# First loads on a second queue, the correction column inside the warm-up, bias rows mirrored at once, and VectorE's half evictions put behind the next minima

## The chip, the cores and the metric

The kernel runs on one core of a Trainium2 chip. The metric is the device time of one execution in microseconds, median of the runs shown. The engines are TensorE (PE in the profile, its weight loads PEld), VectorE (DVE), ScalarE (ACT), GpSimd (POOL) and SyncE (SP), which here only issues transfers. TensorE's clock has two levels in the records, 1.2 and 2.4 GHz; the profile gives it as a share of full, 0.50 or 1.00.

## What is computed

An attention layer with a learned bias over relative positions, followed by two gated feed-forward layers. Batch 2, 8 heads, 576 positions, head size 64; the layers have 1152 tokens, width 512, inner width 1536. Cut to what matters:

```
psi_rel = log1p(|i - j|);  psi_i = log1p(max(i, 1))
x       = psi_rel / psi_i                         # 576 x 576
h       = max(x * w1 + b1, 0)                     # 32 hidden values for each i, j
bias    = h @ w2                                  # one value for each head, i, j
scores  = q @ k.T / 8 + bias
p       = exp(scores - rowmax);  p = p / (rowsum + 1e-9)
y       = p @ v
y       = (sigmoid(y @ w_gate) * (y @ w_val)) @ w_out             # first layer
y       = rmsnorm(y) ... (silu(y @ w_gate) * (y @ w_val)) @ w_out  # second layer
```

## The kernel before

Every engine's instructions are in the order in which the program writes them; nothing is reordered. The work comes in four stages: a warm-up with the first loads, a prelude that makes bias rows, the attention loop, and the two feed-forward layers.

**Loads.** At the start SP issues, in this order: the first part of the table of log distances (`w1l`, four parts), the parameters `prms`, the per-position column `bpr`, the factors `nip`, the table's second part, then the q and k tiles `raw` of four (batch, head pair) combinations, each as two transfers of 64 partitions (one half holds one head; which half comes first alternates with the batch, `half`), and the table's last two parts. VectorE multiplies the table by `w1` (`table`), and `bpr` by `b1` into `bpc`; GpSimd does the same for its own use into `nbpc`.

**Warm-up.** TensorE runs 11 products of a tile of ones (line 133). After them come two tiny products (line 694) of the weights with the column b1, the *correction column*: rows whose hidden values GpSimd made are short of a constant, which VectorE copies into `corr` (lines 695 and 696) and which is added when a bias row is evicted.

**Bias rows.** The 576 positions i are cut into 36 groups T of 16. For a group, four tiles of hidden values `ht` are made (`bias_h`, lines 212, 214 and 216, split over ScalarE, GpSimd and VectorE), then TensorE multiplies them by w2 (`bias_mm`, line 234), and the PSUM result is scaled and shifted into a tile `be`. Because the bias depends on |i - j|, only the wider side of a row is computed; the other side is its mirror image (`bias_end`, lines 258 and 260, on ScalarE for the first 16 groups and on GpSimd for the rest), after which SP stores the tile in DRAM (`bias_d`, line 264). Groups wider than 512 columns are computed in two halves; ScalarE evicts both (line 239), except in groups 0 to 3, where VectorE evicts the second half (line 243). `bias_step` does one step of this pipeline: hidden values of one group, products of the group before, mirror and store of the group before that. So a group is mirrored one step after its eviction. 16 groups are made in the prelude (18 steps), with `qk_mm(0)` and the first bias load after step 9; the other 20 inside the loop. Groups are taken in the order 18 to 23, 16, 17, 8 to 15, 0 to 7, 24 to 35. The pools hold 12 tiles of hidden values, 8 of `be` and 4 PSUM banks for single products.

**Attention loop.** A unit n is one batch, two heads and a block of 128 rows i. For each unit and head, TensorE makes scores (`qk_mm`, line 334, issued one unit ahead), VectorE adds the bias tile `bt` and takes the row minimum of the negated sum (`reduce_min`, line 344, "the minima"), ScalarE takes exponentials (`expo`, line 363), VectorE or GpSimd normalizes (`normal`), TensorE transposes (`transp`, line 390) three units later and multiplies by v (`pv`, line 425). There are two double banks for scores, so the scores of unit n+1 wait for the minima of unit n. The bias tile comes back from DRAM (`load_bias`, line 305) on SP's queue and waits for the stores of its block's eight groups. The order within a unit is a string of letters: M0 and M1 are the minima, X0 and X1 the exponentials, N the normalization of the unit before, Q the next scores, T, E0 to E2 the transposes and their evictions, A, b and c a `bias_step` (two of them in units 0 to 4), B the feeding of bias tiles, L loads, P0, P1 and V the products with v. For units below 20 it is

```
"M0 M1 T X0 N Q E0 E2 E1 A L X1 P0 P1 b c B V"
```

Groups 0 to 3, those with VectorE's half evictions, have their products in units 0 (one), 1 (two) and 2 (one). A half eviction stands in VectorE's queue right behind the hidden values of the next group, and ahead of the next unit's minima or of one more group's hidden values.

Of the kernel before, what the change touches and what calls it, by code (L numbers as in the profile page):

```python
# [13 lines left out]
ALU = mybir.AluOpType  # L14
# [3 lines left out]
B, H, S, D = 2, 8, 576, 64  # L18
# [11 lines left out]
WARM = 11  # L30
SCALE = 1.0 / 8.0
# [8 lines left out]
NORM_DVE = range(6)  # L40

BIAS_HALF_DVE = (0, 1, 2, 3)
PRE = 16

MIRROR_ACT = 16
# [10 lines left out]
LASTV = {22 + i: (i % 2, i // 2) for i in range(8)}  # L56

ORDERS = [
# [3 lines left out]
]  # L62
# [11 lines left out]
def groups_of(it):  # L74
    a, r = BLK[it]
    return range(a // 16, (a + r) // 16)
# [11 lines left out]
def fused_kernel(ctx: ExitStack, tc: tile.TileContext, qk, vp, tab, pcol, invp, prm, wts, rg, out):  # L88
    nc = tc.nc
# [8 lines left out]
    def bank(nm):  # L98
        return ps1.tile([128, 512], F32, tag="one", name=nm)
# [10 lines left out]
    w1l = bp.tile([128, TABW], F32, name="w1l")  # L110
# [3 lines left out]
    corr = bp.tile([128, 3], F32, name="corr")  # L114
    nip = bp.tile([128, 36], F32, name="nip")
    prms = bp.tile([128, 34], F32, name="prms")
    ones = const.tile([128, 128], F32, name="ones")
# [1 line left out]
    nc.vector.memset(corr, 0.0)  # L119

    PARTS = [slice(192, S), slice(S, 1024), slice(0, 192), slice(1024, TABW)]
    nc.sync.dma_start(w1l[:, PARTS[0]], tab[:, PARTS[0]])
    nc.sync.dma_start(prms, prm)
    nc.sync.dma_start(bpr, pcol)
    nc.sync.dma_start(nip, invp)
    ident = const.tile([128, 128], F32, name="ident")
    make_identity(nc, ident)
    rgs = const.tile([128, NCC], F32, name="rgs")


    warm = bank("warm")
    for _ in range(WARM):
        nc.tensor.matmul(warm[:, :128], ones, ones, start=True, stop=True)

    bias_d = [dram.tile([rows_of(i) * H + H, bias_width(i)], F32, name=f"bias_d{i}") for i in range(5)]
# [7 lines left out]
    def half(b, h):  # L143
        x = (h + b) % 2 * 64
        return slice(x, x + 64)

    def load_raw(b, hp):
        t = wk.tile([128, 2, S], F32, tag=f"raw{hp // 2}", name=f"raw{b}{hp}", bufs=4)
        raws[b, hp] = t
        for h in range(2):  # L150
            r = half(b, h)
            nc.sync.dma_start(t[r], qk[b, hp][:, r, h].rearrange("w p s -> p w s"))

    vs = {}

# [24 lines left out]
    nc.sync.dma_start(w1l[:, PARTS[3]], tab[:, PARTS[3]])  # L180
    nc.gpsimd.tensor_scalar(nbpc, bpr, prms[:, 1:2], -1.0, op0=ALU.mult, op1=ALU.mult)
    nc.vector.tensor_scalar(bpc, bpr, prms[:, 1:2], None, op0=ALU.mult)

    def table(i):
        x = w1l[:, PARTS[i]]
        nc.vector.tensor_scalar(x, x, prms[:, 0:1], None, op0=ALU.mult)
# [34 lines left out]
    def bias_mm(T):  # L221
        hs = hts.pop(T)
        c0, w = span(T)
        right = T * 16 + 15
        if GORDER.index(T) in SPARE:
            be = wk.tile([128, 2 * S], F32, tag="raw1", name=f"be{T}", bufs=4)[:, : S + 15]
        else:
            be = bp.tile([128, S + 15], F32, tag="be", name=f"be{T}", bufs=8)
        o = right + c0
        cut = w if w <= 512 else w // 2  # L230
        for a in range(0, w, cut):
            ps = bank(f"bps{T}_{a}")
            for cg in range(4):
                nc.tensor.matmul(  # L234
                    ps[cg * 32 : cg * 32 + 32, :cut], prms[:, 2:34], hs[cg][:, a : a + cut], start=True, stop=True
                )
            off = corr[:, pooled[T] : pooled[T] + 1]
            if not (a and T in BIAS_HALF_DVE):
                nc.scalar.activation(
                    be[:, o + a : o + a + cut], ps[:, :cut], AF.Identity, bias=off, scale=nip[:, T : T + 1]  # L240
                )
            else:
                nc.vector.tensor_scalar(
                    be[:, o + a : o + a + cut], ps[:, :cut], nip[:, T : T + 1], off, op0=ALU.mult, op1=ALU.add
                )
        bes[T] = be

    def bias_end(T):
        be = bes.pop(T)
        c0, w = span(T)  # L250
        right = T * 16 + 15
        if c0 == 0:
            src, dst = be[:, right + 1 : 2 * right + 1][:, ::-1], be[:, :right]
        else:
            k = S - 1 - 16 * T
            src, dst = be[:, right - k : right][:, ::-1], be[:, right + 1 : right + 1 + k]
        if GORDER.index(T) < MIRROR_ACT:
            nc.scalar.activation(dst, src, AF.Copy)
        else:
            nc.gpsimd.tensor_scalar(dst, src, 1.0, 1.0, op0=ALU.mult, op1=ALU.mult)  # L260
        it = IT_OF[T]
        a = sum(BLK[it]) - 1 - right
        r = (T - groups_of(it)[0]) * 128
        nc.sync.dma_start(bias_d[it][r : r + 128, a : a + S + 15], be)
        stored.append(T)

    GORDER = [T for it in ITS for T in groups_of(it)]
    GORDER = GORDER[2:8] + GORDER[:2] + GORDER[8:]
    hq, mq, eq = list(GORDER), [], []


    def bias_step(more=True):
        m, e = mq[:1], eq[:1]
        if hq and more:
            T = hq.pop(0)
            bias_h(T, *BIAS_H[GORDER.index(T)])
            mq.append(T)
        for T in m:
            bias_mm(mq.pop(0))
            eq.append(T)  # L280
        for T in e:
            bias_end(eq.pop(0))


# [28 lines left out]
    def feed_bias(last, wait=0):  # L313
        while ahead and ahead[0] <= last:
            it = UNITS[ahead[0]][2]
            seen = stored[: len(stored) - wait]
            if any(T not in seen for T in groups_of(it)):
                return
            load_bias(ahead.pop(0))
# [369 lines left out]
                idle += 1  # L689


    cps = bank("cps")
    for c in (64, 96):
        nc.tensor.matmul(cps[c : c + 32, :1], prms[:, 2:34], prms[:, 1:2], start=True, stop=True)
    nc.vector.tensor_scalar(corr[96:, 1:2], cps[96:, :1], 1.0 / SCALE, None, op0=ALU.mult)
    nc.vector.tensor_scalar(corr[64:, 2:3], cps[64:, :1], 1.0 / SCALE, None, op0=ALU.mult)
    for i in range(PRE + 2):
        bias_step(i < PRE)
        if i == 3:
# [8 lines left out]
    for n in range(NU + TL + 1):  # L708
        if n == NU:
            attn.close()  # L710
            open_ring("me", range(EARLY, EARLY + MORE), "left")
        ev = []
        on_dve = (2,) if n < NBIAS or n >= NU else (1, 2)

        def evac(i):
            if len(ev) > i:
                if i in on_dve:
                    nc.vector.tensor_copy(*ev[i])
                else:
                    nc.scalar.activation(*ev[i], AF.Copy)  # L720

        def load_new():
            if n in LOADR:
                load_raw(*LOADR[n])
            if n in LOADV:
                load_v(*LOADV[n])
            if n in LASTV:
                load_last(*LASTV[n])

        live = n < NU  # L730
        nb = BSTEPS.get(n, 0)
        acts = {
            "M0": lambda: live and reduce_min(n, 0),
            "M1": lambda: live and reduce_min(n, 1),
            "X0": lambda: live and expo(n, 0),
            "X1": lambda: live and expo(n, 1),
            "T": lambda: 0 <= n - TL < NU and ev.extend(transp(n - TL)),
            "E0": lambda: evac(0),
            "E1": lambda: evac(1),
            "E2": lambda: evac(2),  # L740
            "N": lambda: 0 <= n - 1 < NU and normal(n - 1),
            "C": lambda: n >= NBIAS + LAG and advance(EARLY if live else EARLY + MORE, 1 if live else 2),
            "B": lambda: live and feed_bias(n + 4),
            "A": lambda: nb > 1 and bias_step(),
            "c": lambda: nb > 2 and bias_step(),
            "b": lambda: nb and bias_step(),
            "L": load_new,
            "Q": lambda: n + 1 < NU and qk_mm(n + 1),
            "P0": lambda: drain(peq, 3),
            "P1": lambda: drain(peq, 2),  # L750
            "V": lambda: 0 <= n - TL < NU and pv(UNITS[n - TL]),
        }
        for x in ORDERS[0 if n < NBIAS else 1 if live else 2].split():
            acts[x]()
        if n == NBIAS - 1:
            assert not eq
            prod.close()
            open_ring("mc", range(EARLY), "right")
            fetch()
        if n >= NU:  # L760
            advance(EARLY + MORE, 1)
        if n == NU:
            while (0, 0, 1) not in wp:
                advance(EARLY + MORE, 1)
            gate_val(0)
# [3 lines left out]
    for s in range(EARLY + MORE, RING):  # L769
        tag, size = ("pt", 9 * 128) if s < EARLY + MORE + 2 else ("v", 1024)  # L770
        t = w2.tile([128, size], F32R, tag=tag, name=f"wv{s}", bufs=2 if tag == "pt" else 8)
# [4 lines left out]
    for s in range(NS + 2):  # L776
# [9 lines left out]
        for half in range(2):  # L786
# [6 lines left out]
            if half == 0:  # L793
                if s < NS and not closing(s - 2):
                    low_part(s)
                if s > 1:
                    l, _, _, f = STEPS[s - 2]
# [5 lines left out]
                while norm_queue and norm_queue[0][0] <= s:  # L803
                    _, c, stage, box = norm_queue.pop(0)
# [71 lines left out]
```

## Time and profile before

| | us |
|---|---|
| median of 3 runs | 651.62 |
| lowest and highest | 650.72, 652.21 |
| the profiled execution | 651.69 |
| its span, first to last instruction | 649.9 |
| TensorE busy in the span | 637.6 |
| VectorE, ScalarE, GpSimd busy | 487.3, 352.6, 210.5 |

The profiled execution is within 0.1 us of the median, so its rows can be taken for the kernel's time as they are. Some 1.8 us lie around the span. The mean granted clock of TensorE is 0.989 of full. A group's idle time counts only where its engine holds up the others; the rows below say for each wait what ended it.

### The profile page before, as it was taken

What the parts mean: (1) busy time and instruction counts of PE and PEld (TensorE: products, weight loads), DVE (VectorE), ACT (ScalarE), POOL (GpSimd) and SP (SyncE); (2) the same over time, 40 slices, a digit from 0 to 9 for tenths busy, and PEclk for the clock granted to TensorE, in tenths of its full rate; (3) what the DMA queues carried; (4) which work ended last, traced back from release to release, by engine and by line L of the source; (5) the groups of instructions that cost most, each with busy time, mean ns of one, the idle gap of its engine ahead of it and who ended that gap; (6) DMA issues with size and microseconds to landing.
All of it is one profiled execution on the core that took longest, in us unless ns stands there. A gap on an engine that the chain in (4) does not pass through costs nothing.

```text
span 649.9 us, 11776 instructions
## 1 busy us (share of the span) xinstructions
PE 637.6 (98%) x4450; PEld 575.7 (89%) x4450; DVE 487.3 (75%) x972; ACT 352.6 (54%) x745; POOL 210.5 (32%) x237
## 2 busy tenths in 40 slices
PE   8889999999999999999999999999999999999997
PEld 5235766777799999999999999999999999999997
DVE  6869798688969987889887888787877878431322
ACT  4749888888885663454534545454555535111110
POOL 5401577566664332243322321010323423100000
PEclk9969999999999999999999999999999999999999
DMA  8865956683323342433333410211423322000111
GB/s 190 284 221 174 234 152 210 185 288 103 85 58 126 128 120 79 127 100 106 121 97 98 130 65 34 66 66 32 121 91 115 98 97 66 1 1 1 49 49 48
DMA packets 28472, 71.73 MB, mean 110 GB/s; under 512 B 3840, under 2 KB 6912, under 8 KB 28416
## 3 DMA queue, kind: packets, MB, share of 16 engines
q1 hardware_dynamic: 27552, 69.80, 35.5%
q10 hardware_dynamic: 864, 1.18, 0.5%
q8 instruction: 35, 0.57, 0.4%
q14 instruction: 21, 0.17, 0.1%
HBM read 57.72 MB, written 13.25 MB: 109 GB/s over the span
## 4 chain that ended last, share of the span: by engine, by line
PE 93%; DVE 1%; issue 1%; ACT 0%; DVEq 0%
PE gv L526 47%; PE s L334 7%; PE pv L425 6%; PE tp L390 6%; PE bps L234 3%; PE acc122a L556 1%; PE acc102b L556 1%; PE acc100b L556 1%; PE acc121b L556 1%; PE acc101b L556 1%; PE acc120b L556 1%; PE acc030b L556 1%; PE acc032b L556 1%; PE acc112b L556 1%; PE acc111b L556 1%; PE acc110b L556 1%
## 5 line engine op out<-in xcount | busy, mean ns | idle before, releaser
L503 POOL TENSOR_TENSOR ff<-ff,wr 128x512 int32<-128x512 int32 x72 | 114.1, 1585 | 256.9 <-DVE ff L502 132.9
L532 DVE TENSOR_TENSOR g<-gv,sg 128x384 f32<-128x384 f32 x72 | 40.1, 556 | 90.9 <-PE gv L526 76.9
L534 ACT ACTIVATE gh<-g 128x384 fp32r<-128x384 f32 x72 | 37.8, 525 | 99.2 <-DVE g L532 99.2
L526 PE MATMUL gv<-nh,wv 128*128 128x384 f32 x288 | 76.5, 337 | 0.0
L526 PE MATMUL gv<-xh,wh 128*128 128x384 f32 x216 | 73.2, 339 | 0.0
L526 PE MATMUL gv<-xl,wh 128*128 128x384 f32 x216 | 72.9, 337 | 0.0
L526 PE MATMUL gv<-xh,wl 128*128 128x384 f32 x216 | 72.8, 337 | 0.0
L493 DVE TENSOR_SCALAR ff<-wr 128x512 uint32<-128x512 uint32 x72 | 63.2, 877 | 0.0
L530 ACT ACTIVATE sg<-gv 128x384 f32<-128x384 f32 x72 | 34.5, 479 | 44.8 <-PE gv L526 44.8
L344 DVE CUSTOM_DVE_ANT_0 t<-s,bt 128x576 f32<-128x576 f32 x72 | 51.4, 751 | 9.6 <-PE s L334 7.6
L363 ACT ACTIVATE p<-t,mn 128x576 f32<-128x576 f32 x72 | 55.2, 767 | 4.1 <-DVE mn L344 4.1
L334 PE MATMUL s<-raw 64*128 64x288 f32 (+1 forms) x320 | 49.7, 439 | 5.7 <-issue 3.2
L507 ACT ACTIVATE wh<-ab 128x512 fp32r<-128x512 f32 x42 | 26.5, 631 | 52.2 <-DVE ab L506 51.8
L216 DVE TENSOR_SCALAR ht<-w1l,bpc 128x304 f32<-128x304 f32 (+17 forms) x100 | 53.0, 593 | 0.1
L526 PEld LDWEIGHTS gv<-nh,wv 128*128 128x128 f32 x288 | 52.4, 188 | 0.0
L540 DVE TENSOR_TENSOR gl<-g,gh 128x384 fp32r<-128x384 f32 x72 | 45.5, 631 | 7.0 <-ACT gh L534 7.0
L506 DVE SCALAR_TENSOR_TENSOR ab<-ab,ff 128x512 f32<-128x512 f32 x72 | 49.3, 685 | 1.2 <-POOL ff L503 1.2
L502 DVE SCALAR_TENSOR_TENSOR ff<-wr,ff 128x512 uint32<-128x512 uint32 x72 | 49.8, 692 | 0.0
L377 POOL TENSOR_SCALAR p<-p,rs 128x576 f32<-128x576 f32 x60 | 48.5, 820 | 2.2 <-DVE rs L372 2.2
L526 PE MATMUL gv<-nh,wh 128*128 128x384 f32 x144 | 48.7, 338 | 0.0
L526 PE MATMUL gv<-nl,wh 128*128 128x384 f32 x144 | 48.6, 337 | 0.0
L526 PE MATMUL gv<-nh,wl 128*128 128x384 f32 x144 | 48.6, 337 | 0.0
(363 smaller groups left out, 1569.9 us busy)
## 6 DMA issues: line engine op xcount, KB each, us to landing
wr<-wts SPq DMA_DIRECT2D x72, 512.0 KB, 3.6
bias_d<-be SPq DMA_DIRECT2D x36, 295.5 KB, 4.2
bt<-bias_d SPq DMA_DIRECT2D x16, 576.0 KB, 5.0
raw<-qk SPq DMA_DIRECT2D x16, 288.0 KB, 6.9
v<-vp SPq DMA_DIRECT2D x8, 320.0 KB, 4.0
bt<-bias_d SPq DMA_DIRECT2D x8, 144.0 KB, 2.9
out<-part SPq DMA_DIRECT2D x6, 192.0 KB, 1.8
out<-part ACTq DMA_DIRECT2D x6, 192.0 KB, 1.9
```

Source lines behind the costliest of these rows:

```text
L216: nc.vector.tensor_scalar(ht, src, bpc[:, t : t + 1], 0.0, op0=ALU.add, op1=ALU.max)
L334: nc.tensor.matmul(dst[:, hf, :288], raw[r, 0, r0 : r0 + rows], raw[r, 1, cs], start=True, stop=True)
L344: nc.vector.tensor_tensor_reduce(t, sp[:, :, :288], bt[:, 0 if UNITS[n][0] is None else j].rearrange("p (a c) -> p a c", a=2), -SCALE, 3.0e38,
L363: nc.scalar.activation(p[:, j], t.rearrange("p a c -> p (a c)"), AF.Exp, bias=mn[:, j : j + 1], scale=-1.0, accum_out=sm[:, j : j + 1],)
L377: nc.gpsimd.tensor_scalar(p[:, j], p[:, j], rs[:, j : j + 1], 1.0, op0=ALU.mult, op1=ALU.mult)
L493: nc.vector.tensor_scalar(ff, hw, 3, 0x3FFFFFFF, op0=ALU.logical_shift_left, op1=ALU.bitwise_and)
L502: nc.vector.scalar_tensor_tensor(ff, hw, 0xC0000000, ff, op0=ALU.bitwise_and, op1=ALU.bitwise_or)
L503: nc.gpsimd.tensor_tensor(ff.bitcast(I32), ff.bitcast(I32), lw.bitcast(I32), op=ALU.add)
L506: nc.vector.scalar_tensor_tensor(ab, ab, TINY_HI, ff.bitcast(F32), op0=ALU.is_ge, op1=ALU.mult)
L526: nc.tensor.matmul(ps[:, :CH], wt[:, cs], xt[:, cc, :], start=(k == 0), stop=(k == 11))
L540: nc.vector.tensor_tensor(gl, g32, gh.bitcast(F32), op=ALU.subtract)
L556: nc.tensor.matmul(dst, st_[:, m * 128 : m * 128 + 128], mv, start=(head and k == 0), stop=(last and k == 2))
```

## The change

Four edits. First, the table's first part, the factors `nip`, and the second half of each of the four early q and k loads are issued by ScalarE's queue instead of SP's. Second, the correction column's two products come after 5 of the 11 warm-up products, and VectorE's two copies of it right after the scaling of `bpr`. Third, the first 16 groups are mirrored and stored in the same step as their eviction. Fourth, VectorE's half evictions are put on a list, which is worked off at the start of the next `bias_step` or at a new letter D, behind the two minima, whichever comes first. The diff:

```
-    "M0 M1 T X0 N Q E0 E2 E1 A L X1 P0 P1 b c B V",
+    "M0 M1 D T X0 N Q E0 E2 E1 A L X1 P0 P1 b c B V",
...
-    nc.sync.dma_start(w1l[:, PARTS[0]], tab[:, PARTS[0]])
+    nc.scalar.dma_start(w1l[:, PARTS[0]], tab[:, PARTS[0]])
     nc.sync.dma_start(prms, prm)
     nc.sync.dma_start(bpr, pcol)
-    nc.sync.dma_start(nip, invp)
+    nc.scalar.dma_start(nip, invp)
...
-    for _ in range(WARM):
+    for _ in range(WARM // 2):
+        nc.tensor.matmul(warm[:, :128], ones, ones, start=True, stop=True)
+    cps = bank("cps")
+    for c in (64, 96):
+        nc.tensor.matmul(cps[c : c + 32, :1], prms[:, 2:34], prms[:, 1:2], start=True, stop=True)
+    for _ in range(WARM - WARM // 2):
         nc.tensor.matmul(warm[:, :128], ones, ones, start=True, stop=True)
...
-            nc.sync.dma_start(t[r], qk[b, hp][:, r, h].rearrange("w p s -> p w s"))
+            q = nc.scalar if h and hp < 2 else nc.sync
+            q.dma_start(t[r], qk[b, hp][:, r, h].rearrange("w p s -> p w s"))
...
     nc.vector.tensor_scalar(bpc, bpr, prms[:, 1:2], None, op0=ALU.mult)
+
+    nc.vector.tensor_scalar(corr[96:, 1:2], cps[96:, :1], 1.0 / SCALE, None, op0=ALU.mult)
+    nc.vector.tensor_scalar(corr[64:, 2:3], cps[64:, :1], 1.0 / SCALE, None, op0=ALU.mult)
...
-                nc.vector.tensor_scalar(
-                    be[:, o + a : o + a + cut], ps[:, :cut], nip[:, T : T + 1], off, op0=ALU.mult, op1=ALU.add
-                )
+                late.append((be[:, o + a : o + a + cut], ps[:, :cut], nip[:, T : T + 1], off))
...
+    late = []
+
+    def bias_rest():
+        while late:
+            nc.vector.tensor_scalar(*late.pop(0), op0=ALU.mult, op1=ALU.add)
...
     def bias_step(more=True):
+        bias_rest()
...
         for T in e:
             bias_end(eq.pop(0))
+        if eq and GORDER.index(eq[0]) < AT_ONCE:
+            bias_end(eq.pop(0))
...
-    cps = bank("cps")
-    for c in (64, 96):
-        nc.tensor.matmul(cps[c : c + 32, :1], prms[:, 2:34], prms[:, 1:2], start=True, stop=True)
-    nc.vector.tensor_scalar(corr[96:, 1:2], cps[96:, :1], 1.0 / SCALE, None, op0=ALU.mult)
-    nc.vector.tensor_scalar(corr[64:, 2:3], cps[64:, :1], 1.0 / SCALE, None, op0=ALU.mult)
...
+            "D": bias_rest,
```

`AT_ONCE` is 16.

## Rows read from the trace of the kernel before

**Rows 1.** Windows of TensorE: stretch, us, busy (instructions), clock, DMA share, GB/s.

```profile
0.00:55.00 55.00, 46.28 (x293) 0.88 0.79 233
55.00:650.00 595.00, 591.31 (x4159) 1.00 0.32 99
```

**Rows 2.** Windows of units 0, 1, 2: PE, PEld, DVE, ACT, POOL, clock, DMA.

```profile
28.77:34.63 5.86, 4.42 (x24) 1.63 (x24) 4.49 (x11) 3.94 (x9) 0.22 (x1) 0.68 1.01 369
34.63:42.69 8.06, 6.30 (x40) 3.11 (x40) 6.05 (x18) 3.99 (x8) 0.48 (x2) 0.59 0.73 235
42.69:49.74 7.05, 6.20 (x40) 3.08 (x41) 5.44 (x17) 3.99 (x8) 0.26 (x1) 0.76 0.40 132
```

**Rows 3.** Timeline of VectorE: start, us, line, operation, [idle before <- releaser].

```profile
34.14 0.58 DVE L243 TENSOR_SCALAR be<-bps,nip,corr 128x288 f32<-128x288 f32 x1 [1.37 <-ACT be L239]
...
40.51 0.57 DVE L243 TENSOR_SCALAR be<-bps,nip,corr 128x280 f32<-128x280 f32 x1 [1.94 <-PE bps L234]
...
48.11 0.55 DVE L243 TENSOR_SCALAR be<-bps,nip,corr 128x264 f32<-128x264 f32 x1 [1.54 <-PE bps L234]
```

**Rows 4.** Timeline of VectorE from the start to the first minima.

```profile
4.23 0.29 DVE L182 TENSOR_SCALAR bpc<-bpr,prms 128x144 f32<-128x144 f32 x1 [3.23 <-DMA bpr<-pcol]
4.44 0.55 DVE L186 TENSOR_SCALAR w1l<-w1l,prms 128x384 f32<-128x384 f32 x1
6.36 0.16 DVE L695 TENSOR_SCALAR corr<-cps 32x1 f32<-32x1 f32 x1 [1.37 <-PE cps L694]
...
6.75 3.56 DVE L216 TENSOR_SCALAR ht<-w1l,bpc 128x304 f32<-128x304 f32 x10
...
28.77 0.76 DVE L344 CUSTOM_DVE_ANT_0 t<-s,bt 128x576 f32<-128x576 f32 x1 [1.94 <-DMA bt<-bias_d]
```

**Rows 5.** Timeline of SP's queue: start, us until the last issue's end.

```profile
1.65 0.42 SPq L124 DMA_DIRECT2D bpr<-pcol  x1
...
11.36 9.43 SPq L264 DMA_DIRECT2D bias_d<-be  x8
```

**Rows 6.** Transfers issued at 1.65, 20.47 and 24.49: KB, us to landing.

```profile
bpr<-pcol SPq DMA_DIRECT2D x1, 72.0 KB, 2.5
...
bias_d<-be SPq DMA_DIRECT2D x1, 295.5 KB, 3.9
...
bt<-bias_d SPq DMA_DIRECT2D x1, 576.0 KB, 4.3
```

**Rows 7.** Timeline of TensorE: warm-up, scores at half and at full clock.

```profile
1.05 5.06 PE L133 MATMUL warm<-ones 128*128 128x128 f32 x22 [1.05 <-DVE corr L119]
...
35.49 2.93 PE L334 MATMUL s<-raw 64*128 64x288 f32 x8 [1.48 <-issue]
...
50.56 1.91 PE L334 MATMUL s<-raw 64*128 64x288 f32 x8 [0.48 <-DVE mn L344]
```

**Rows 8.** Timeline of ScalarE: evictions 8 and 9, and the mirror behind the ninth.

```profile
17.01 0.60 ACT L239 ACTIVATE be<-bps,corr,nip 128x304 f32<-128x304 f32 x1 [0.35 <-PE bps L234]
...
19.39 0.72 ACT L239 ACTIVATE be<-bps,corr,nip 128x448 f32<-128x448 f32 x1 [1.46 <-PE bps L234]
20.01 0.43 ACT L258 ACTIVATE be<-be 128x287 f32<-128x287 f32 x1
```

**Rows 9.** Windows: early half loads, a 128-partition load, two later half loads.

```profile
8.00:15.00 7.00, 6.84 (x54) 3.41 (x52) 7.00 (x17) 4.33 (x10) 5.09 (x8) 1.00 1.05 219
...
42.44:43.21 0.77, 0.00 (x0) 0.00 (x0) 0.77 (x2) 0.00 (x0) 0.00 (x0) 1.00 1.01 387
83.50:84.40 0.90, 0.90 (x11) 0.17 (x10) 0.90 (x4) 0.59 (x2) 0.08 (x1) 1.00 0.98 278
```

**Rows 10.** Windows of TensorE: the two spells at half clock.

```profile
30.90:41.10 10.20, 8.72 (x52) 0.50 0.79 265
...
44.60:48.00 3.40, 3.40 (x26) 0.50 0.31 97
```

More of the change, by code (lines that the diff above doesn't have):

```diff
@@ L42 @@
 BIAS_HALF_DVE = (0, 1, 2, 3)
+AT_ONCE = 16
 PRE = 16
```

## The prediction

> **What bounds the kernel now.** I read the page first, then the busy time by stretches, then the three iterations at the seam by timelines, then the loads. TensorE is what the time consists of: from 55 us on it is busy 591.31 of 595 us at the full clock, while in the first 55 us it is busy only 46.28 and its granted clock averages 0.88 [rows 1]. So whatever makes the first 55 us shorter should come off the end, and the change touches only that part. There the reader should see two things. Units 0, 1 and 2 of the attention loop take 5.86, 8.06 and 7.05 us, with VectorE idle 1.4 to 2.0 us in each [rows 2]; the idle time stands in front of the half evictions of line 243, 1.37, 1.94 and 1.54 us [rows 3]. VectorE runs into an eviction whose product TensorE has not finished, and the next minima, which TensorE's next scores wait for, stand behind it. And before unit 0, VectorE computes hidden rows without a pause from 6.75 to 26.83 and then waits 1.94 us for the first bias tile [rows 4].
>
> **Start of VectorE.** Constants and correction column. The column operand bpr is issued at 1.65 us and lands 2.5 later; the scaling that needs it starts at 4.23 [rows 4 to 6]. With the table's first part gone to ScalarE's queue, bpr moves up one issue slot, 0.47 us, so the scaling can start at 3.76. Before, VectorE scaled, prepared the table (0.55) and then stood 1.37 us until the correction product at the end of the warm-up was there, and started the first hidden row at 6.75 [rows 4]. Now that product sits behind 5 of 11 warm-up products: 1.05 + 5/11 of 5.06 = 3.35 us [rows 7], so it is there when VectorE asks. The new order is scaling 0.21, two corrections 0.20 each, table 0.55: 3.76 + 0.21 + 0.40 + 0.55 = 4.9. If the new traffic on the second queue delays bpr by the slot that it gained, 5.4. I take 5.05: 1.7 us sooner. The 20.1 us of hidden rows then end at 25.1 instead of 26.83. The other six warm-up products end about 0.3 us later than before, at 6.4, still ahead of the old start of bias products.
>
> **First bias tile.** Before, the eight stores are issued from 11.36 to 20.47 [rows 5]; the last lands 3.9 us after its issue and the bias tile 4.3 us after its own [rows 6]: 20.5 + 3.9 + 4.3 = 28.7, which is the 28.77 of the first minima. "Mirrored at once" sends each store when its own eviction is done and not one row later: the eighth eviction starts at 17.01 [rows 8], now 15.3, with its 0.60 and a mirror of 0.4 done at 16.4. The mirror now reads what the instruction just ahead of it on ScalarE writes. No row here shows that tie; untied neighbours overlap by 0.1 us (20.01 against 19.39 + 0.72) [rows 8], so it costs from nothing, if they still overlap, to about 0.2 each, the overlap and as much again, and I take 0.1. ScalarE's own waits for TensorE cover it (0.35 and 1.46 in these rows); without them sixteen mirrors would be 1.6 us. SP's queue gets one store more ahead of the bias load, the ninth: its eviction moves from 19.39 to 17.7, mirrored by 18.9, issued by 19.2. So the bias load goes out at max(19.2, 16.5 + 3.9 = 20.4) and lands at 24.7, just before 25.1. That holds if the transfers are not backed up.
>
> **Are they?** From 8 to 15 us the queue moves 219 GB/s with the engines' share at 1.05, all of it half loads (64 partitions each); a load over 128 partitions runs at 387 GB/s with the same share, and in one later place two half loads queued together moved 278 [rows 9]. The stores stand behind these loads. With the two halves in two queues the load phase (eight of 288 KB, 2.36 MB, 10.8 us at 219) takes 8.5 us at 278 and 6.1 at 387. For a bias tile at 25.1 the eighth store has to land by 20.8 instead of 24.4: 3.6 us of relief. The first half load goes out three issue slots sooner, 1.4 us; at 278 GB/s 2.3 more come, 3.7 in all. I take it that the halves overlap at least that well, since the late pair did; no row shows two queues, so the other end (no overlap) is a rival below. The Trainium skill's page "SBUF — State Buffer", section "Can I just issue two DMAs to hit both halves?", says the reverse: two transfers, one on each half of the partitions, serialize, with a gain of 6% measured. Its page "DMA: Bandwidth & Descriptors", section "Issuing engines are not separate DMA queues", adds that a second issuing engine saves only issue time. By that rule the time is that of the second rival, 647.7.
>
> **The six issues on ScalarE** take 0.42 us for a small one [rows 5]; with twice that for the four half loads (an estimate) they are 4.2 us and end near 5, while the first product that ScalarE could evict starts behind the warm-up, at 6.4. ScalarE's idle time hides them; without it they would be those 4.2 us.
>
> **Half evictions.** In units 0, 1 and 2 they now come behind the next minima, or behind the next hidden rows.
> Unit 0: the wait (1.37) and the eviction (0.49) go: 5.86 - 1.86 = 4.0.
> Unit 1: one eviction (0.49) comes in behind the minima, one (0.48) leaves: VectorE reached the remaining one 3.94 us after its minima began (40.51 - 1.94 - 34.63), now at 4.43. TensorE delivered at 5.88, at half clock (its eight score products take 2.93 us there, 1.91 at full [rows 7]). At half clock 1.45 us of wait are left, at full none: 8.06 - 1.94 = 6.1, up to 7.6.
> Unit 2: by the same sum it is reached at 4.36 instead of 3.88 against a delivery at 5.42: 7.05 - 1.54 + 0.48 = 6.0, up to 7.1.
> The bank that a late eviction holds is next wanted by a product a unit later; nothing queues for it. POOL's mirror and SP's store of these four rows follow the eviction, and their tile is read in unit 8, so they have time.
> Sum: the minima of unit 3 begin at 25.1 + 4.0 + 6.1 + 6.0 = 41.2 (all full) to 43.8 (all half). The clock did fall to half here, for 10.2 us with 8.72 of them busy and for 3.4 us under unbroken work [rows 10]; TensorE's gaps get shorter but stay, so I take the middle, 42.4, against 49.74: 7.3 us sooner.
> Before, all from unit 3 on ran at full clock. Now a spell at half can reach into it, where TensorE has no gaps and pays: 0 to 1.7 us (half of 3.4), I take 1.0. **Gain 6.3 us.**
>
> From there TensorE paces everything, and VectorE, ScalarE and the transfers move with it. The profiled execution took 651.69, the median is 651.62, so nothing is to be corrected: 651.7 - 6.3 = **645.4**. Its own range: all at full clock 651.7 - 8.7 = 643.0, all at half with the late start 651.7 - 3.9 = 647.8.
>
> **Rivals.**
> Second: the halves don't overlap. Then the loads gain only their 1.4 us of earlier issue, the eighth store lands at 24.4 - 1.4 = 23.0, the bias tile at 27.4, and VectorE waits 2.3 us at 25.1: 647.7 (645.5 to 649.5). For it: 219 GB/s with all engines at 1.05. Against: the 278.
> Third, no change: what is won is lost later, to a transfer that does not move up with the rest. It has to be 6 us; TensorE idles only 3.7 us in all after 55, and the transfers' share there is 0.32 [rows 1]. 651.5.
> Fourth, slower: with the gaps shorter but more even, the clock stays at 1.2 GHz through units 3 to 6, where TensorE has no gaps. Each us there loses half a us. 12.6 us at half cancel the gain, 15.2 make it measurably slower, 18 give 651.7 - 7.3 + 9 = 653.4. For it: 8.72 busy us of 10.2 did not bring the clock back sooner. Against: the spell under unbroken work ended after 3.4.
>
> **How the numbers follow.** Chances 0.57, 0.31, 0.06 and 0.06. The first two are faster by over 0.2% (1.3 us, about what this measurement can tell from no change): 0.88; within it 0.06; slower 0.06. The range, 643.2 to 648.7, takes in the first case and nearly all of the second; the third and fourth and the tails lie outside.
>
> **What would show it.** Right: first hidden row near 5.0; no wait for the bias tile; about 4 us between the minima of units 0 and 1; no wait in front of line 243 at full clock; the minima of unit 3 near 42.4; the same busy TensorE afterwards. Wrong: stores still landing near 23 us (second rival), a long stretch at half clock after unit 3 (fourth), or new idle time of TensorE after 55 us (third).

## The result, and the profile after

The changed kernel takes 645.89 us (median of 4 runs, 645.52 to 646.31), the kernel before 651.81 with the runs made beside it. The ratio is 0.9918, with a 95% interval of 0.9899 to 0.9936: 0.8% faster. The profiled execution took 646.31, its span is 644.5. The forecast was 645.4, range 643.2 to 648.7. One run below, of the kernel with useless products, took 696.65 us at a mean clock of 0.851, where its other five took 646.8 to 647.66 at 0.999 and 1.000; the ratio given for it is of those five.

VectorE's timeline up to the first minima (as [rows 4]):

```profile
3.65 0.29 DVE L189 TENSOR_SCALAR bpc<-bpr,prms 128x144 f32<-128x144 f32 x1 [2.64 <-DMA bpr<-pcol]
3.97 0.17 DVE L191 TENSOR_SCALAR corr<-cps 32x1 f32<-32x1 f32 x1
...
4.36 0.42 DVE L196 TENSOR_SCALAR w1l<-w1l,prms 128x384 f32<-128x384 f32 x1
4.82 5.11 DVE L226 TENSOR_SCALAR ht<-w1l,bpc 128x304 f32<-128x304 f32 x10
...
22.99 2.77 DVE L226 TENSOR_SCALAR ht<-w1l,bpc 128x368 f32<-128x368 f32 x7
28.27 0.76 DVE L361 CUSTOM_DVE_ANT_0 t<-s,bt 128x576 f32<-128x576 f32 x1 [2.50 <-DMA bt<-bias_d]
```

The first hidden row starts at 4.82 instead of 6.75, but the hidden rows end only 1.07 us sooner, at 25.76, and the first minima begin at 28.27 instead of 28.77: the wait for the bias tile grew from 1.94 to 2.50 us. The windows say why (units 0, 1 and 2, then the early loads; columns as in [rows 2]):

```profile
28.27:32.19 3.92, 3.10 (x12) 1.49 (x16) 3.92 (x11) 2.95 (x6) 0.00 (x0) 0.72 0.99 352
32.19:38.51 6.32, 5.64 (x56) 2.21 (x48) 6.05 (x18) 4.54 (x9) 0.76 (x3) 0.90 0.67 203
38.51:44.41 5.90, 5.04 (x37) 2.38 (x38) 5.83 (x18) 3.81 (x8) 0.62 (x2) 1.00 0.96 343
8.00:15.00 7.00, 7.00 (x45) 2.05 (x42) 7.00 (x17) 5.50 (x12) 5.33 (x9) 1.00 1.05 222
```

From 8 to 15 us the transfers move 222 GB/s, against 219 on one queue [rows 9]. Units 0 to 2 take 3.92, 6.32 and 5.90 us, 16.14 together, against 20.97 [rows 2]. So of the 5.38 us by which the two profiled executions differ, 4.83 are gained in these three units, 0.50 ahead of them, and after them the distances stay. The 0.50 is no more than the spread of single profiles: with the same half loads on two queues, the first minima begin at 27.80, 28.35 and 28.95 in three variants below, and at 28.76 with the loads of the kernel before. Now TensorE (by windows, as [rows 1], then the one spell at half clock and what follows, as [rows 10]):

```profile
0.00:55.00 55.00, 49.05 (x344) 0.97 0.83 250
55.00:644.00 589.00, 585.87 (x4110) 1.00 0.33 98
...
30.00:33.40 3.40, 3.40 (x22) 0.50 1.04 398
33.50:60.00 26.50, 24.84 (x210) 1.00 0.65 212
```

The clock is at half for 3.4 us instead of 13.6, and at full from 33.4 us on, early in unit 1. TensorE idles 3.1 us after 55, before it was 3.7.

The SP queue and the two transfers that matter (as [rows 5, 6]; the store is the eighth, issued at 17.38, the tile at 24.15):

```profile
9.94 9.80 SPq L278 DMA_DIRECT2D bias_d<-be  x9
24.15 0.89 SPq L322 DMA_DIRECT2D bt<-bias_d  x2
```

```profile
bias_d<-be SPq DMA_DIRECT2D x1, 295.5 KB, 6.7
...
bt<-bias_d SPq DMA_DIRECT2D x1, 576.0 KB, 4.1
```

The eighth store is sent 3.1 us sooner and takes 6.7 us instead of 3.9: it lands at 24.1, 0.3 sooner. It stood behind the stores ahead of it, and those behind the loads: by issue and landing the last half load was there at 16.4 and the last part of the table at 16.8, the first store at 17.4, and the others followed one after another.

### The profile page after: what moved, and what is told of

It is laid out like the page before. It is cut to its first block, busy times and chain, and to the rows that moved or that the text cites. A ratio compares the mean times of both kernels' runs of the same rounds, so it can differ in the third digit from the quotient of the medians.

```text
span 644.5 us, 11776 instructions
## 1 busy us (share of the span) xinstructions
PE 634.9 (99%) x4450; PEld 572.6 (89%) x4450; DVE 487.8 (76%) x972; ACT 354.3 (55%) x745; POOL 212.1 (33%) x237
## 4 chain that ended last, share of the span: by engine, by line
PE 91%; DVE 5%; DMA 2%; ACT 1%; issue 1%; SPq 0%; DVEq 0%
PE gv L543 44%; PE s L351 6%; PE pv L442 6%; PE tp L407 6%; PE bps L244 4%; DMA bias_d<-be 1%; DVE ff L510 1%; DVE ht L226 1%; PE acc122a L573 1%; PE acc102b L573 1%; PE acc100b L573 1%; PE acc120b L573 1%; PE acc121b L573 1%; PE acc101b L573 1%; PE acc030b L573 1%
## 5 line engine op out<-in xcount | busy, mean ns | idle before, releaser
L351 PE MATMUL s<-raw 64*128 64x288 f32 (+1 forms) x320 | 47.8, 431 | 3.9 <-DVE mn L361 2.5
```

Of the source, the lines that this page charges most:

```text
L351: nc.tensor.matmul(dst[:, hf, :288], raw[r, 0, r0 : r0 + rows], raw[r, 1, cs], start=True, stop=True)
```

## The experiments

Theory A: the half evictions' place makes the gain by itself, and the prelude's edits are hidden behind the bias tile. Theory B: the sum as predicted, with some 3.6 us from the prelude. Theory C came up after the first runs: the evictions' place matters because TensorE's gaps bring its clock down. Kernels run on the same chip share their runs of the kernel before, whose median was 650.4 in the first group, 651.14 in the second and 650.49 in the third; each ratio below is to those.

**One edit undone at a time.**

Half evictions back at their place:

```
-                late.append((be[...], ps[:, :cut], nip[:, T : T + 1], off))
+                nc.vector.tensor_scalar(be[...], ps[:, :cut], nip[:, T : T + 1], off, op0=ALU.mult, op1=ALU.add)
```

> The changed kernel with VectorE's half evictions back at their old place, everything else kept. Theory A (the half evictions carry the gain; the prelude ends when the first bias tile lands, which the other edits moved by only 0.5 us): units 0 to 2 take about 20.5 to 21 us again instead of 16.1, so about 650.7 us (650.0 to 651.5). Theory B (the sum as predicted: the prelude edits bring 3.6 us, the evictions the rest): about 648.2.

Measured 649.62 (12 runs, 645.25 to 651.43), ratio 0.9983 (0.9967 to 0.9998). Against its own runs of the kernel before it is 0.8 us faster, which is nearer A than B, though the time itself lies 0.4 us below A's range. But the spread is what tells: the run of 645.25 had a mean clock of 1.000 and, in the old order, was as fast as the changed kernel; the one of 651.43 had 0.988. Its profile has the waits in front of the evictions again, 1.55 and 1.89 us, and TensorE at half clock around them; up to 34.3 us, through all of unit 0, the clock was full, and it fell after TensorE's own gap there (VectorE's timeline, one line of TensorE's, then windows with columns as in [rows 2]):

```profile
38.98 0.57 DVE L253 TENSOR_SCALAR be<-bps,nip,corr 128x280 f32<-128x280 f32 x1 [1.55 <-PE bps L244]
...
46.92 0.55 DVE L253 TENSOR_SCALAR be<-bps,nip,corr 128x264 f32<-128x264 f32 x1 [1.89 <-PE bps L244]
```

```profile
34.35 2.54 PE L351 MATMUL s<-raw 64*128 64x288 f32 x8 [1.45 <-issue]
```

```profile
35.50:38.80 3.30, 3.30 (x26) 1.32 (x26) 1.93 (x5) 1.04 (x3) 0.09 (x1) 0.50 0.30 66
42.30:49.00 6.70, 6.70 (x35) 2.70 (x34) 4.74 (x14) 3.34 (x8) 0.26 (x1) 0.50 0.47 172
```

Correction column back behind the warm-up (its two products and VectorE's two copies again ahead of the first bias step):

> The changed kernel with the correction column back behind the warm-up. VectorE's first hidden row should start near 6.2 instead of 4.8. Theory A: the hidden rows end near 27.2, still ahead of the first bias tile at 28.2, so no change: 645.9 within 0.5. Theory B (VectorE's start sets the prelude): 1.4 us slower, 647.3.

Measured 645.98, ratio 0.9929 (0.9915 to 0.9942): no change, as A has it. Its VectorE timeline:

```profile
6.71 3.61 DVE L221 TENSOR_SCALAR ht<-w1l,bpc 128x304 f32<-128x304 f32 x10
...
27.80 0.76 DVE L356 CUSTOM_DVE_ANT_0 t<-s,bt 128x576 f32<-128x576 f32 x1 [1.37 <-DMA bt<-bias_d]
```

VectorE starts its hidden rows 1.9 us later than in the changed kernel and still waits 1.37 us for the tile. The first ten hidden rows take 3.61 us here and 5.11 in the changed kernel; more on that below.

Mirrors one step later:

```
-AT_ONCE = 16
+AT_ONCE = 0
```

> The changed kernel with the first 16 bias rows mirrored one step after their eviction again. Theory A: the stores queue behind the half loads either way; the eighth store is issued near 18.7 and still lands near 24, so no change beyond 0.5 us: 645.9. Theory B: the bias tile moves by the step that the mirror moves, about 1.2 us: 647.1.

Measured 645.75, ratio 0.9931 (0.9917 to 0.9944): no change.

All first loads on SP's queue:

```
-    nc.scalar.dma_start(w1l[:, PARTS[0]], tab[:, PARTS[0]])
+    nc.sync.dma_start(w1l[:, PARTS[0]], tab[:, PARTS[0]])
...
-    nc.scalar.dma_start(nip, invp)
+    nc.sync.dma_start(nip, invp)
...
-            q = nc.scalar if h and hp < 2 else nc.sync
+            q = nc.sync
```

> The changed kernel with all first loads on SyncE's queue again. Theory A: half loads run near 220 GB/s on one queue or two, so the bias tile moves by 0.5 us, the earlier start of the loads: 646.4 (645.9 to 646.9). Theory B (two queues relieve the transfers as predicted): the tile lands 3.6 us later: 649.

Measured 647.5, ratio 0.9951 (0.9937 to 0.9965): 1.5 to 1.8 us slower than the two runs above, which shared its chip, and between the theories. In its profile (648.06, against 646.31 for the changed kernel) the first minima begin at 28.94, 0.67 later. That is what A expects, but single profiles spread as much. Another 1.05 us are in unit 1, which takes 7.37 us instead of 6.32: TensorE is at half clock there, and the wait in front of the half eviction comes in the new order too:

```profile
38.53 0.57 DVE L260 TENSOR_SCALAR be<-bps,nip,corr 128x280 f32<-128x280 f32 x1 [1.25 <-PE bps L244]
```

The mean clock was 0.994 in three of six runs against 0.997 to 0.999 in the changed kernel's. Why it falls for longer here was not tried.

**One edit alone.** The kernel before with the half evictions moved and nothing else:

```
-                nc.vector.tensor_scalar(
-                    be[...], ps[:, :cut], nip[:, T : T + 1], off, op0=ALU.mult, op1=ALU.add
-                )
+                late.append((be[...], ps[:, :cut], nip[:, T : T + 1], off))
...
+            "D": bias_rest,
```

> The kernel before with only VectorE's half evictions moved behind the next minima. Theory A: units 0 to 2 take 16.1 to 16.5 us instead of 20.97, from 28.8 on: 646.9 (646.2 to 647.6). Theory B (two thirds of the gain come from the prelude): 649.3.

Measured 647.08, ratio 0.9937 (0.9924 to 0.9951): A's value. This one edit gives 4.1 of the 5.3 us that the whole change gives against the same median (0.9918 of 651.14 is 645.8); the 1.2 us between them are not clear of the noise, since the intervals overlap. Units 0 to 2 in its profile (columns as in [rows 2]) run at full clock throughout:

```profile
28.76:32.68 3.92, 3.10 (x24) 1.70 (x24) 3.92 (x10) 3.12 (x7) 0.00 (x0) 1.00 1.00 358
32.68:38.71 6.03, 4.80 (x41) 2.10 (x40) 5.96 (x17) 4.25 (x9) 0.78 (x3) 1.00 0.71 239
38.71:44.61 5.90, 5.04 (x37) 2.37 (x38) 5.83 (x18) 3.81 (x8) 0.62 (x2) 1.00 0.95 326
```

**Order or clock?** The kernel before, in its own order, with products that nobody reads where TensorE waits:

```
+    def fill(n):
+        t = bank(f"fill{n}")
+        for _ in range(8):
+            nc.tensor.matmul(t[:, :128], ones, ones, start=True, stop=True)
...
-            "Q": lambda: n + 1 < NU and qk_mm(n + 1),
+            "Q": lambda: (n < 3 and fill(n), n + 1 < NU and qk_mm(n + 1)),
```

> The kernel before, in its own order, with eight products of the tile of ones (their result is read by nobody) on TensorE ahead of the scores of units 1, 2 and 3, where it waits for VectorE. Theory C (the half evictions cost mainly because TensorE's waits bring its clock down, which makes VectorE wait longer): the mean clock rises from 0.991 to 0.998 or more and the time falls to 647.3, where a straight line through the 25 runs of the kernel before, time against mean clock, ends at full clock; 646.8 to 648.5. Theory A (the order of VectorE's queue by itself costs the 4.8 us): 650 or more, whatever the clock.

Measured 647.18, ratio 0.9942 (0.9921 to 0.9962), mean clock 0.999 to 1.000 in five of six runs: theory C. Units 0 to 2 in its profile, then the first of the three groups of useless products:

```profile
29.61:34.15 4.54, 3.72 (x30) 2.37 (x30) 4.49 (x11) 3.43 (x7) 0.22 (x1) 1.00 1.00 376
34.15:40.21 6.06, 6.06 (x62) 4.37 (x61) 5.99 (x18) 3.94 (x8) 0.36 (x2) 1.00 0.66 188
40.21:45.66 5.45, 5.45 (x47) 3.15 (x46) 5.38 (x17) 3.56 (x8) 0.37 (x2) 1.00 1.01 379
```

```profile
27.42 2.05 PE L711 MATMUL fill<-ones 128*128 128x128 f32 x16
```

The three units take 16.05 us in the old order, as much as in the new one (16.14), although TensorE does 6 us of useless work in and ahead of them, and VectorE idles 0.2 us in 16 (it was 5.0 in 20.97). At full clock TensorE has the product ready when VectorE comes to its eviction. So theory A in its plain form falls: in this kernel the order costs 4.8 us only together with a lowered clock. Which gap lowers it the run does not say, for the first group fills the wait for the bias tile ahead of unit 0, and the other two the waits inside the units. Both kinds occur: in the kernel before the clock falls at 30.9 [rows 10], ahead of the first late eviction; with the half evictions undone (above) it falls only after a gap inside the units.

**What holds the early loads.** Each q and k tile by one transfer over 128 partitions, from an input in which the two halves of a tile are rows of one array (the host rearranges, the bytes and the 2304-byte runs stay):

```
-        for h in range(2):
-            r = half(b, h)
-            q = nc.scalar if h and hp < 2 else nc.sync
-            q.dma_start(t[r], qk[b, hp][:, r, h].rearrange("w p s -> p w s"))
+        nc.sync.dma_start(t, qk[b, hp].rearrange("w p s -> p w s"))
```

> The changed kernel with each early and late q and k tile loaded by one transfer over all 128 partitions on SyncE's queue, from an input laid out so that a tile's two halves are rows of one array (same bytes, same 2304-byte runs). If the 64 partitions are what holds the loads to 220 GB/s: the load phase runs near 390, the eighth store lands near 19, the first bias tile before VectorE's hidden rows end at 25.8, no wait in front of the first minima: 2.3 to 2.5 us faster than the changed kernel, 643.5. If something else holds it (reading memory, the number of queues): 645.9 within 0.5.

Measured 643.52 (4 runs, 643.49 to 643.61), ratio 0.9882 (0.9869 to 0.9896): by the ratios 2.3 us faster than the changed kernel, and the fastest version here together with one variant below. Windows from 4 to 12 us and VectorE's timeline:

```profile
4.00:8.00 4.00, 4.00 (x29) 3.03 (x29) 3.87 (x10) 1.51 (x2) 2.77 (x6) 1.00 0.99 357
8.00:12.00 4.00, 3.37 (x27) 0.94 (x20) 4.00 (x8) 3.63 (x8) 3.94 (x6) 1.00 1.04 391
```

```profile
22.89 2.76 DVE L223 TENSOR_SCALAR ht<-w1l,bpc 128x368 f32<-128x368 f32 x7
25.68 0.76 DVE L358 CUSTOM_DVE_ANT_0 t<-s,bt 128x576 f32<-128x576 f32 x1
```

391 GB/s on one queue, and no wait ahead of the first minima: the state that the prediction had expected of the two queues.

The same input layout, but half loads on two queues as in the changed kernel (the load reads `qk[b, hp][:, r]`):

> The changed kernel, half loads on two queues, but from the other input layout, in which the rows of a half are next to one another. If the partitions hold the rate: 222 GB/s from 8 to 15 us as before, 645.9 within 0.5. If the gaps between the rows in memory hold it: near 390 GB/s and 643.5.

Measured 646.4, ratio 0.9926 (0.9913 to 0.9938), and

```profile
8.00:15.00 7.00, 6.37 (x56) 2.06 (x47) 7.00 (x16) 5.68 (x13) 5.83 (x9) 1.00 1.06 230
```

so it is the 64 partitions and not the distance of the rows in memory. Nor is it that a half load is smaller: the load over 128 partitions that moved 387 GB/s [rows 9] is of 320 KB, a half load of 288.

Loads divided by head pair, so that both queues should hold the same half at the same time:

```
-            q = nc.scalar if h and hp < 2 else nc.sync
+            q = nc.scalar if hp == 1 else nc.sync
```

> The changed kernel with its early half loads divided over the two queues so that both queues load the same 64 partitions at the same time (one head pair each). If opposite halves in two queues overlap at all, this loses it: the eighth store lands a us or more later and the time is about 647. If two queues never overlap their halves: about 222 GB/s from 8 to 15 us and 645.9 within 0.5.

Measured 645.38 (644.68 to 647.54), ratio 0.9921 (0.9901 to 0.9941), and

```profile
8.00:15.00 7.00, 6.77 (x48) 2.06 (x42) 7.00 (x16) 5.69 (x10) 5.33 (x10) 1.00 1.07 237
```

The loss that overlapping halves would have brought did not come; the first minima even begin at 26.90 in its profile. But the two queues did not hold equal halves throughout. If each queue serves its loads one after another, as their landings suggest, they drifted apart: ScalarE's first load was sent at 3.4 us, and from 8.4 to 10.5 and from 11.4 to 13.3 the halves were opposite after all. In the changed kernel they were opposite from 8.7 to 9.9 and equal from 9.9 to 12.2. The windows of these stretches, of the changed kernel and then of this run:

```profile
8.70:9.90 1.20, 1.20 (x8) 0.42 (x8) 1.20 (x4) 0.72 (x2) 0.41 (x1) 1.00 1.06 225
9.90:12.20 2.30, 2.30 (x16) 0.57 (x14) 2.30 (x6) 1.95 (x4) 1.99 (x3) 1.00 1.05 234
...
8.40:10.50 2.10, 2.10 (x16) 0.63 (x16) 2.10 (x6) 1.32 (x2) 1.00 (x3) 1.00 1.05 247
11.40:13.30 1.90, 1.90 (x16) 0.54 (x15) 1.90 (x5) 1.84 (x5) 1.33 (x3) 1.00 1.07 201
```

In these stretches opposite halves move 201 to 247 GB/s and equal ones 234, all far below 387: the two queues did not overlap their halves in either kernel.

**The other edits with the loads out of the way.** Whole-tile loads with the column back behind the warm-up:

> Whole-tile loads, and the correction column back behind the warm-up. If the wait for the bias tile is what swallowed VectorE's earlier start, the start counts here: 1.3 to 1.5 us slower than whole-tile loads with the early column, about 644.9. If the start never mattered: equal to whole-tile loads, 643.5.

Measured 645.25 (643.91 to 646.04), ratio 0.9903 (0.9888 to 0.9919). The median is near the expectation, but not by the expected path: in its profile, which took 643.91, the hidden rows start 1.46 us later (6.34) and the minima only 0.43 (26.11). The runs with a mean clock of 0.997 to 0.999 took 645.25 to 646.04, those with 1.000 took 643.91 and 643.95. So 0.4 us are VectorE's start, and the rest went with the clock in these five runs. The mean clock alone does not set it: runs of the next variant at 0.999 took 643.62 and 643.77.

Whole-tile loads with the mirrors a step later:

> Whole-tile loads, with the first 16 bias rows mirrored one step later again. With the loads out of the way the eighth store should now be as late as it is issued, near 19 instead of 17.1, and the bias tile should land near 26.5 against hidden rows that end at 25.65: 0.6 to 1.2 us slower than whole-tile loads, 644.1 to 644.7. If mirroring at once is hidden here too: 643.5.

Measured 643.62, ratio 0.9889 (0.9871 to 0.9907): a miss, nothing is lost. The eighth store is sent at 19.36, as expected, but it lands 2.2 us after its issue, where it took 3.4 behind its neighbour when they came closer, and the tile is there at 25.7 (4.1 us after 21.64), with the end of the hidden rows. The store:

```profile
bias_d<-be SPq DMA_DIRECT2D x1, 295.5 KB, 2.2
```

Whole-tile loads with the half evictions at their old place:

> Whole-tile loads, with VectorE's half evictions back at their old place. Theory A: as between the kernel before and its variant with the evictions moved alone, 4.1 us slower than whole-tile loads: 647.6, in every run. Theory C: the time goes with the clock of the run: runs with a mean clock of 1.000 within 1 us of 643.5, those at 0.99 near 648.

Measured 647.89 (646.63 to 648.42), ratio 0.9951 (0.9933 to 0.9969). By their times both theories allow it: 4.3 us slower than the variant above, in runs whose mean clock was 0.992 to 0.995, and no run stayed at full clock. But its profile (646.63, mean clock 0.995) shows that the clock is not all. Unit 0 ran at full clock and took 5.59 us, 1.67 more than the 3.92 of whole-tile loads with the new order. Its window, VectorE's wait, and TensorE's product behind a wait of its own:

```profile
25.79:31.38 5.59, 4.48 (x34) 1.66 (x30) 4.50 (x12) 5.45 (x12) 0.00 (x0) 1.00 1.02 380
```

```profile
30.88 0.58 DVE L250 TENSOR_SCALAR be<-bps,nip,corr 128x288 f32<-128x288 f32 x1 [1.09 <-ACT p L377]
```

```profile
29.59 1.17 PE L241 MATMUL bps<-ht,prms 128*32 128x288 f32 x14 [0.46 <-ACT ht L219]
```

The profile names ScalarE's exponential as what ended the wait, but the product itself ended only at 30.76. Read from this profile, and not tested by itself: with no wait for the bias tile ScalarE is still mirroring the last rows of the prelude, and its hidden values reach TensorE late. So where something else makes the product late, the old order costs time at full clock too.

## Why the prediction was right, and where it was not

The time was right to 0.5 us, by the mechanism that was named for the units (VectorE queued behind an eviction whose product is late). That it was so close is luck: one step failed (3.2 us too much ahead of unit 0), two terms were too cautious (some 2.2 us together), and they nearly cancel. The time also lies in the range of the second rival, 645.5 to 649.5.

- **Start of VectorE.** Right in kind: 4.82 measured, 5.05 taken. Its worth was oversized: VectorE started 1.93 us sooner, and 1.07 were left at the end of the hidden rows, with slower rows where GpSimd makes its own at the same time (last section). None of it counted, as undoing the column shows (645.98).
- **First bias tile: the step that failed.** "I take it that the halves overlap at least that well" is wrong: 222 GB/s, not 278 or more, and the tile came at 28.25 instead of the 24.7 that was taken. Of the 3.67 us ahead of unit 0 (28.77 to 25.1) only 0.50 came. The second rival's premise is what happened, and it was still too kind: not 1.4 us of relief but 0.3, since the loads ended at 16.83 instead of 17.41 and the stores behind them landed one after another. The Trainium skill's page "SBUF — State Buffer", section "Can I just issue two DMAs to hit both halves?", says that two such transfers serialize, and this trace agrees: two queues gave 222 against 219 GB/s. The late pair at 278 was no evidence: it was a window of 0.9 us in one queue, and the 0.9 us ahead of it moved 213 GB/s.
- **Half evictions.** 3.92, 6.32 and 5.90 us against 4.0, 6.1 to 7.6 and 6.0 to 7.1: right, at the end of the range with full clock. The waits of 1.45 and 1.06 us that half clock would have left did not come; 0.20 did.
- **The clock.** The middle value cost 1.2 us in the units (42.4 against 41.2), and 1.0 was set aside behind them: about nothing was measured for either. The prediction treated the clock as something that the change meets. The run with useless products shows that it is most of what the change buys: with TensorE's gaps filled the clock stays full, and then the old order waits 0.2 us in these units. That the new order keeps the clock because its gaps are shorter fits this, but is argued; and with whole-tile loads the old order waits at full clock too.
- **Mirrored at once.** Sent earlier, though less than forecast (the eighth at 17.38, before 20.47, forecast 16.5); worth nothing, not even with the loads out of the way.
- **From unit 3 on.** Right: the shift stays, 5.3 us at unit 3, 5.38 at the end.

With the measured terms the sum is 0.50 + 4.83, 5.3 us against 6.3. The third and fourth rivals did not come.

Open: when exactly the clock falls. Runs of one kernel differ in it (645.25 to 651.43 in one case); after the wait of about 2.5 us ahead of unit 0 it fell at 30.0 in the changed kernel's profile and stayed full in that of the half evictions moved alone. With it stays open why undoing the queue edit costs over 1.5 us.

## What to carry to other kernels

Before a wait is costed, look at the clock in that window: a wait of TensorE can lengthen the next one, so that an order that costs next to nothing at full clock costs microseconds (here 16.05 against 20.97 us for three units). Then look at it again when something else has moved: the same order cost 1.67 us at full clock behind a shorter prelude. Two half-partition transfers in two queues did not make a whole one (222 against 391 GB/s); lay the data out so that one transfer covers all partitions. An edit ahead of a transfer that everybody waits for is worth what the transfer gains, and should be tried again once the transfer is out of the way.

## What the runs showed of the hardware

VectorE's rows of hidden values were slower while GpSimd worked on its own: the first ten take 5.11 us in the changed kernel, where both start together, and 3.61 in the one with the column at its old place, where VectorE starts 1.9 us later. In the changed kernel GpSimd's seven run from 4.96 to 9.11 without a gap:

```profile
4.96 4.15 POOL L224 TENSOR_SCALAR ht<-w1l,nbpc 128x304 f32<-128x304 f32 x7 [0.77 <-DVE w1l L196]
```

In the kernel with the column at its old place GpSimd stands idle from 6.75 to 8.52, and VectorE's rows that start in that time take 0.37 to 0.39 us each; in the changed kernel the median of those up to 8 us is 0.65.

No run changed GpSimd's part alone, so the link is read from the overlap and not shown by itself.

One kernel spreads by 6 us from run to run where TensorE's gaps are longer (half evictions undone, twelve runs, mean clock 0.988 to 1.000), another by 0.12 us where they are shorter (whole-tile loads, four runs, mean clock 1.000 each).
